# First batch's k and q loaded by groups of four heads, first attention block in two parts, attention times v in 64x64 tiles from block 8 and two blocks later, and new planner costs

## The chip, the cores and the metric

The kernel runs on one core of one Trainium2 chip. The metric is the device time in microseconds (us) of one execution, as the median of several runs. The engines are TensorE (PE, with its weight loads as PEld), VectorE (DVE), ScalarE (ACT), GpSimd (POOL) and SyncE (SP), which here issues nearly all DMAs.

## What is computed

Sliding-window attention, and then a two-layer feed-forward with a squared ReLU on its output:

```python
B, H, S, D = q.shape                                    # 8, 8, 576, 64
scores = np.matmul(q, k.transpose(0, 1, 3, 2)) / np.sqrt(D)
mask = np.abs(pos[:, None] - pos[None, :]) <= 32
scores = np.where(mask, scores, -1e9)
attn = np.exp(scores - scores.max(-1, keepdims=True))
attn = attn / (attn.sum(-1, keepdims=True) + 1e-9)
x = np.matmul(attn, v).transpose(0, 2, 1, 3).reshape(B * S, H * D)   # 4608 x 512
r = np.maximum(x @ w_in, 0.0)                           # 4608 x 2048
out = (s * (r * r) + b) @ w_out                         # 4608 x 512
```

All inputs and the output are float32 in DRAM. The kernel multiplies in bfloat16.

## The kernel before

The 4608 tokens are cut into 36 attention blocks of 128 tokens. A block's result is written, transposed, into a slot of the tile xt (512 features x 128 tokens). The feed-forward takes tokens in tiles of 128 (six tiles) and then 256 (fifteen). Its first product (line 1015) writes 512 columns of ht; ACT applies the ReLU (line 1024), DVE squares into gt (line 1043); the second product (line 1063) sums 16 matmuls per 128 tokens into one of the banks outp and ptp (in the last tiles also sc and av), DVE scales and adds the constant row cvec (line 1077), and SP stores. cvec is b times the column sums of w_out; the matmuls called quarters (line 940) need all of w_out. The feed-forward alone is 1344 + 592 matmuls. It fixes most of PE's work, and the rest of PE's time is attention, transposes and waiting.

Attention comes in three forms. (1) The first LIGHT = 3 blocks go through `attend_light`: scores and transposed scores are both computed, the row maxima are turned on PE and subtracted there, ACT takes the exponential of the transposed scores, and the normalised result is turned back (lines 691 to 782). (2) The other blocks go through `attend`: scores (line 820), a mask-and-maximum on DVE (line 832) and an exponential on ACT (line 840) for each of eight heads, a division by the row sums in two halves on POOL or DVE (line 854), and a transpose of the probabilities p into pts, on PE for the blocks below PDMA = 4 (line 877) and by a DMA after that (line 868). (3) The product with v is `av_one` for blocks below NOLD = 12: sixteen matmuls with 128 contracted rows, for which a copy vo of v shifted by 64 rows is made by `make_vo` (line 892). From block 12 on it is `av` in 64x64 tiles: 24 small matmuls into two banks (lines 909 and 915), one of which ACT copies to half (line 924) before DVE adds both into xt (line 926).

The first batch's k and q (blocks 0 to 3 use nothing else) come raw. Each is loaded in two halves, which split the 36 rows of a chunk: 16 chunks by 8 heads on the partitions (lines 571 and on). Each half is cast to bfloat16 (to parts of xt) and turned by matmuls with a permutation (line 593) into kwt and qwt, five banks for each. A block's scores need all five banks of both, and so all four loads. Later k and q are loaded in 128-token rows, cast (line 551, to kn and qn), and turned on PE up to block 11 (line 667, eight transposes each) and by a DMA after that.

The weights come in eight loads of 1 MB, i0 to i3 of w_in and o0 to o3 of w_out. Each is staged in a slot of gt (o2 in the output buffer) and cast in four pieces of 128x512. The order of the loads is the string FIRST: K and Q are the raw halves, `|` separates what is asked for before block 0, after block 0, after block 1 and so on. All loads are issued by SP in that order, each behind the one before it.

The order on every engine is worked out on the host, before launch, by a list scheduler (class `_Plan`). Every operation has a cost in ns for each engine that may run it, a latency, a key (its due position, mostly the token number minus a lead), and the resources that it reads and writes. On a free engine the ready operation of the smallest key goes next. An operation with several allowed engines is put where it would start and end first. The plan is then the fixed order of that engine: at run time each engine goes through its list and waits on semaphores, so an operation that comes late holds back everything behind it on its engine. A flag "small" on scores and tiled `av` makes the plan put them next to each other (HOLD, DEFER). Where the plan sees PE idle in the early stages it inserts dummy matmuls (`fill`, line 462).

Of the kernel before, what the change touches and what calls it, by code (L numbers as in the profile page):

```python
# [62 lines left out]
class _Plan:  # L63
# [39 lines left out]
    def order(self):  # L103
# [8 lines left out]
        def room(t, nd):  # L112

            while sum(q * min(1.0, (end - t) / dur) for end, dur, q in queue if end > t) + nd > RING:
                t += 50.0
            return t
# [15 lines left out]
        while len(out) < len(self.nodes):  # L132
# [13 lines left out]
            n = min(here, key=lambda m: (m.key, m.nid))  # L146
            if e == "pe":
# [123 lines left out]
def bass_sliding_window_symmetric__then__act_starrelu_kernel(  # L271
# [22 lines left out]
    CKEY, SKEY = 200, -9250  # L294
    SLOT = dict(i0=0, i1=1, i2=2, i3=3, o0=2, o1=3, o2=4, o3=2)
    RAWNS = 1450
    WHOLE, LIGHT, CH, NDIV = 4, 3, S // 16, 5
# [5 lines left out]
    AVK, NOLD, ONE, NVO = 384, 12, 11, 2  # L303

    def akey(j):
        return 128 * j - min(LEAD, L0 + LS * j)


    def CSET(j):
        return ("pool",)  # L310

    def VSET(j):
        return ("pool", "dve")

    def OSET(j):
        return ("act", "dve")

    with ExitStack() as es:
# [6 lines left out]
        def ps(shape, dt, nm):  # L325
# [16 lines left out]
        SS = [sb((128, 4, 128), F32, "ss") for _ in range(NS)]  # L342
        P = [sb((128, 8, 128), BF16, "p") for _ in range(NP)]
# [11 lines left out]
               for x, g in (("K", 0), ("Q", 8))}  # L355
        FLAT = {x: XT[:, :, :].rearrange("p a b -> p (a b)")[:, o:o + CH * D]
                for x, o in (("K", 0), ("Q", CH * D))}
# [3 lines left out]
        PICK = sb((128, 8, 128), BF16, "pick")  # L361
        EPS = sb((128, 128), BF16, "eps")
        M16 = [sb((128, 8, 2), BF16, "m16") for _ in range(2)]
        MT = [sb((16, 128), BF16, "mt") for _ in range(2)]
# [39 lines left out]
        def aff(dst, src, pat, base, cm, fill, rd, wr, key):  # L404
            add("pool", lambda e: e.affine_select(dst, src, pattern=pat, compare_op=ALU.is_ge,
                                                  fill=fill, base=base, channel_multiplier=cm),
                330, key, reads=rd, writes=wr)

        KC = K0 + 20
        for sg in (1, -1):  # L410
            src = ONES[:, 0:128] if sg == 1 else PERM[:, :]
            aff(PERM[:, :].rearrange("p (a g c) -> p a g c", a=2, g=NPAIR),
# [155 lines left out]
        def load_raw(x, half):  # L568
# [5 lines left out]
            if half:  # L574
                turn_raw(x)
# [568 lines left out]
```

## Time and profile before

| | |
|---|---|
| median of 3 runs | 319.31 us (319.23 to 321.96) |
| the profiled execution | 316.46 us |
| its span, first to last instruction | 314.7 us |
| granted clock of TensorE | 1.00 |
| PE busy | 300.8 us, 96% |
| DVE, ACT, POOL busy | 229.0, 230.0, 145.5 us |
| DMA | 61.82 MB, mean 196 GB/s |

The difference between the profiled execution and its span (1.8 us) lies before the first and after the last instruction. Times in the views count from the start of the span. In a row of the timeline stand the start, the length, the engine, the line, the operation, out<-in and the number of instructions merged, and in brackets the idle time before it with what ended it. Matmul rows overlap: the distance from one start to the next tells more than the length.

### The profile page before, as it was taken

Reading aid. Unit: us, or ns where it says so; the run is one execution under the profiler, and the core shown is the slowest. Engines: PE = TensorE matmul, PEld = TensorE weight load, DVE = VectorE, ACT = ScalarE, POOL = GpSimd, SP = SyncE. Lnnn points to the kernel's source line nnn. Section 1 sums busy time; section 2 is a strip of 40 time slices with the busy share of each in tenths; the row PEclk is TensorE's granted clock in tenths of the full one; section 3 lists DMA queues with packets and bytes.
Section 4 is the critical chain, followed back from the end, with each engine's and each line's share of the span. In section 5 each row is a group of like instructions: output and inputs, shape, how many; then the busy total and the mean of one; then the engine's idle time right before and its main releaser. Section 6 shows DMA issues by size and latency. Waiting matters only on the chain.

```text
span 314.7 us, 10141 instructions
## 1 busy us (share of the span) xinstructions
PE 300.8 (96%) x3936; PEld 207.4 (66%) x3981; DVE 229.0 (73%) x897; ACT 230.0 (73%) x747; POOL 145.5 (46%) x192
## 2 busy tenths in 40 slices
PE   7899899998999999999999999999999999999996
PEld 3468657586667665776666766666666666676674
DVE  5779499899998778677766787678858767653242
ACT  5577866899797868698787878798878778835230
POOL 7233476556575534445454654655654532220000
PEclk9999999999999999999999999999999999999999
DMA  7998999999999999999999999899999562220011
GB/s 273 359 351 228 361 268 214 240 229 179 210 213 210 232 187 197 223 227 176 191 218 226 210 205 233 217 192 226 225 247 204 123 149 70 70 67 35 33 69 68
DMA packets 157125, 61.82 MB, mean 196 GB/s; under 512 B 131220, under 2 KB 147988, under 8 KB 157076
## 3 DMA queue, kind: packets, MB, share of 16 engines
q1 hardware_dynamic: 157072, 61.16, 90.7%
q8 instruction: 31, 0.51, 0.7%
q14 instruction: 18, 0.15, 0.2%
q10 hardware_dynamic: 4, 0.00, 0.0%
HBM read 37.03 MB, written 9.44 MB: 148 GB/s over the span
## 4 chain that ended last, share of the span: by engine, by line
PE 77%; DMA 7%; DVE 7%; ACT 3%; POOL 2%; issue 2%; SPq 1%
PE ht L1015 35%; PE ptp L1063 15%; PE outp L1063 15%; DMA gt<-in_moe_w_out_dram 3%; PE sc L820 3%; DMA v<-in_v_dram 2%; ACT p L840 2%; PE sc L1063 2%; DMA r32k<-in_k_dram 2%; PE av L1063 2%; DVE ss L832 1%; PE tp L909 1%; PE av L915 1%; DVE mx L704 1%; DVE outs L1077 1%
## 5 line engine op out<-in xcount | busy, mean ns | idle before, releaser
L1015 PE MATMUL ht<-xt,win 128*128 128x256 bf16 (+1 forms) x1344 | 146.5, 257 | 0.0
L1015 PEld LDWEIGHTS ht<-xt,win 128*128 128x128 bf16 x1344 | 115.1, 98 | 32.7
L1024 ACT ACTIVATE r<-ht 128x512 bf16<-128x512 f32 x144 | 85.1, 592 | 47.3 <-PE ht L1015 45.8
L1043 DVE TENSOR_TENSOR gt<-r 128x512 bf16<-128x512 bf16 x144 | 83.6, 583 | 48.7 <-ACT r L1024 47.1
L840 ACT ACTIVATE p<-ss,mx 128x128 bf16<-128x128 f32 x264 | 110.0, 420 | 7.6 <-DVE mx L832 6.9
L854 POOL TENSOR_TENSOR p<-p,rc 128x512 bf16<-128x512 bf16 x64 | 70.0, 1114 | 77.5 <-DVE rc L849 77.5
L832 DVE CUSTOM_DVE_ANT_0 ss<-sc,mask 128x128 f32<-128x128 f32 x264 | 62.0, 280 | 8.8 <-PE sc L820 8.4
L1063 PE MATMUL outp<-wout,gt 128*128 128x512 bf16 (+1 forms) x246 | 63.0, 372 | 3.9 <-issue 1.7
L1063 PE MATMUL ptp<-wout,gt 128*128 128x512 bf16 x240 | 61.9, 379 | 1.7 <-issue 1.3
L840 ACT ACTIVATION_READ_ACCUMULATOR p<-ss,mx 128x1 f32 x264 | 50.2, 190 | 0.0
L1063 PEld LDWEIGHTS outp<-wout,gt 128*128 128x128 bf16 x272 | 24.9, 98 | 19.3 <-ACT wout L556 1.0
L1063 PEld LDWEIGHTS ptp<-wout,gt 128*128 128x128 bf16 x256 | 24.1, 98 | 19.3
L551 POOL CAST kn<-r32k 128x512 bf16<-128x512 f32 x34 | 21.1, 646 | 23.9 <-DMA r32k<-in_k_dram 23.9
L551 POOL CAST qn<-r32q 128x512 bf16<-128x512 f32 x32 | 21.3, 665 | 9.9 <-DMA r32q<-in_q_dram 9.5
L832 DVE DVE_READ_ACCUMULATOR2_ANT mx<- 128x1 f32 x264 | 20.8, 79 | 0.0
L924 ACT COPY half<-tp 128x512 f32<-128x512 f32 x24 | 14.0, 583 | 9.2 <-PE av L915 8.8
L551 POOL CAST ve<-v 128x512 bf16<-128x512 f32 x27 | 18.0, 667 | 3.3 <-PE av L915 2.5
L926 DVE TENSOR_TENSOR xt<-av,half 128x512 bf16<-128x512 f32 x24 | 16.3, 681 | 0.9 <-ACT half L924 0.8
L820 PEld LDWEIGHTS sc<-kt,qt 64*64 64x64 bf16 x768 | 10.8, 108 | 8.7 <-issue 7.8
L820 PE MATMUL sc<-kt,qt 64*64 64x64 bf16 (+1 forms) x768 | 14.2, 204 | 0.0
L846 DVE TENSOR_SCALAR sm<-sm 128x8 f32<-128x8 f32 x33 | 6.7, 202 | 8.9 <-ACT p L840 8.8
L1077 DVE SCALAR_TENSOR_TENSOR outs<-outp,scb,cvec 128x512 f32<-128x512 f32 (+1 forms) x17 | 12.4, 728 | 0.9 <-PE outp L1063 0.9
(142 smaller groups left out, 237.3 us busy)
## 6 DMA issues: line engine op xcount, KB each, us to landing
out_dram<-outs SPq DMA_DIRECT2D x35, 256.0 KB, 3.8
v<-in_v_dram SPq DMA_DIRECT2D x28, 256.0 KB, 5.5
r32q<-in_q_dram SPq DMA_DIRECT2D x28, 256.0 KB, 5.2
r32k<-in_k_dram SPq DMA_DIRECT2D x9, 512.0 KB, 4.7
gt<-in_moe_w_in_dram SPq DMA_DIRECT2D x4, 1024.0 KB, 10.6
gt<-in_moe_w_out_dram SPq DMA_DIRECT2D x3, 1024.0 KB, 9.7
v<-in_v_dram SPq DMA_DIRECT2D x8, 192.0 KB, 5.1
r32k<-in_k_dram SPq DMA_DIRECT2D x3, 448.0 KB, 4.8
```

The source lines that it names most:

```text
L551: return e.tensor_copy(dst, src)
L820: r = e.matmul(SC[hh][64 * u:64 * u + 64, pr, x0:x1], lhsT=qq, rhs=kk, start=True, stop=True)
L832: lambda e, ss=ss, x=x, y=y, pr=pr, hh=hh: e.tensor_tensor_reduce(out=SS[ss][:, x, :], in0=SC[hh][:, pr, :], in1=MASK[kind][:, :], scale=- ...
L840: lambda e, ss=ss, x=x, y=y: e.activation(P[pb][:, y, :].rearrange("q (a p t) -> q a p t", a=2, t=2), spread(SS[ss][:, x, :]), AF.Exp, bia ...
L854: return e.tensor_tensor(P[pb][:, y0:y0 + 4, :], P[pb][:, y0:y0 + 4, :], RC[mb][:, y0:y0 + 4].unsqueeze(2).broadcast_to([128, 4, 128]), AL ...
L924: add("act", lambda e: e.copy(HALF[hb][:, :], AV2[:, :]), 620, key + AVK, reads=[AV2N], writes=[("HALF", hb)])
L926: add("dve", lambda e: e.tensor_tensor(XT[:, :, 128 * (j % NX):128 * (j % NX) + 128], AV[:, :, :], HALF[hb][:, :].rearrange("p (a b) -> p ...
L1015: r = e.matmul(hbank[:, nt * f:nt * f + nt], lhsT=WIN[:, kc, 128 * ft:128 * ft + 128], rhs=XT[:, kc, x0:x0 + nt], start=(kc == 0), stop=(k ...
L1024: return e.activation(R1[rb][:, :], hbank[:, :], AF.Relu, bias=0.0, scale=1.0)
L1043: return e.tensor_tensor(d, r, r, ALU.mult)
L1063: r = e.matmul(op_[:, 0:cn], lhsT=GT[:, g_, fc, :], rhs=WOUT[:, fc, c0:c0 + cn], start=(fc == 0), stop=(fc == 15))
L1077: add("dve", lambda e, ob=ob, op_=op_, c0=c0, cn=cn: e.scalar_tensor_tensor(OUTS[ob][:, 0:cn], op_[:, 0:cn], SCB[:, 0:1], CVEC[:, c0:c0 + cn],
```

## The change

- **Raw k and q.** The first halves are now heads 0 to 3 and the second halves heads 4 to 7 (32 chunks by 4 heads on the partitions, 18 rows of each, the same bytes in each load). A half can be turned by itself: six groups of twelve matmuls for k and as many for q in place of five groups each. The order is Q0 K0 Q1 K1. The casts go to the buffers of ss and p rather than to xt.
- **Block 0** (`NSPLIT = 1`) is worked in two parts, heads 0 to 3 and heads 4 to 7, each with its own scores, maxima, exponential, product and normalisation. Block 1 is cut in the two sets of even and odd heads. The row sums now share a bank with the product. LIGHT falls from 3 to 2, so block 2 goes through `attend`.
- **Loads.** i0 goes ahead of v0 and v1; k2 and o0 go ahead of v3, q4 and v4; q5 ahead of o1. The slots of o0 and o1 are those that i0 and i1 leave.
- **AV.** `NOLD` falls from 12 to 8, so blocks 8 to 11 use 64x64 tiles and have no vo. `attend_av(j - 2)` is asked for after the scores of block j (DA = 2). PDMA rises from 4 to 5: block 4's probabilities are turned on PE.
- **Feed-forward.** Eight tiles of 128 and fourteen of 256; TAIL falls from 3 to 2.
- **Engines.** Weights may be cast on DVE too; v is cast on POOL alone (POOL or DVE before); k and q below block 8 on POOL or ACT (POOL before); vo also on POOL; the division on POOL alone from block 2 (NDIV 5 to 2); ReLU keys 400 ns earlier.
- **Costs.** Nearly all costs and latencies of the planner are new, mostly smaller costs and larger latencies, and the leads LEAD and LS, which makes a new order on every engine. The five dummy operations with the scalars s and b move from the head to after block 1.

In the order that the planner gives out, PE has 10 dummy matmuls (16 before), 144 matmuls of line 593 as before, 24 transposes of p (8 before), 96 matmuls of `av_one` (144 before), and 224 + 448 small ones of `av` (192 + 384 before).

```diff
-START, RING, ISSUE, LAND = 800.0, 2400.0, 700.0, 2000.0
+START, RING, ISSUE, LAND = 800.0, 2400.0, 700.0, 1200.0
-HOLD, DEFER, CHANGE = 800.0, 200.0, 97.0
+HOLD, DEFER, CHANGE = 200.0, 200.0, 97.0
-        n = _Node(len(self.nodes), eng, fn, cost, 300.0 if eng == "pe" else 130.0, key, dsem,
+        n = _Node(len(self.nodes), eng, fn, cost, {"pe": 300.0, "pool": 190.0}.get(eng, 230.0), key, dsem,
...
-    TILES = [128] * 6 + [256] * 15
+    TILES = [128] * 8 + [256] * 14
-    LEAD, L0, LS = 640, 600, 60
-    RELU, SQ = 500, 200
-    FIRST = "K0 K1 Q0 Q1 v0 v1 i0 i1 i2 v2 i3 v3 v4|q4 o0 k2 o1 o2 q5 o3|v5|||"
+    LEAD, L0, LS = 560, 600, 70
+    RELU, SQ = 900, 200
+    FIRST = "Q0 K0 Q1 K1 i0 v0 v1 i1 i2|v2 i3 k2 o0 v3 q4 q5 v4 o1 o2 o3||v5||"
-    WSET = {"i": ("pool", "act"), "o": ("act", "pool")}
-    NFLEX, TAIL = 8, 3
-    PDMA, KQDMA, AHEAD, GATE = 4, 11, 4, 5
-    SLOT = dict(i0=0, i1=1, i2=2, i3=3, o0=2, o1=3, o2=4, o3=2)
-    WHOLE, LIGHT, CH, NDIV = 4, 3, S // 16, 5
+    WSET = {"i": ("pool", "act", "dve"), "o": ("act", "pool", "dve")}
+    NFLEX, TAIL = 10, 2
+    PDMA, KQDMA, AHEAD, GATE = 5, 11, 4, 5
+    SLOT = dict(i0=0, i1=1, i2=2, i3=3, o0=0, o1=1, o2=4, o3=2)
+    RAWNS, NSPLIT = 1450, 1
+    WHOLE, LIGHT, CH, NDIV = 4, 2, S // 16, 2
-    AVK, NOLD, ONE, NVO = 384, 12, 11, 2
+    AVK, NOLD, ONE, NVO, DA = 384, 8, 11, 2, 2
     def CSET(j):
-        return ("pool",)
+        return ("pool",) if j >= 8 else ("pool", "act")
     def VSET(j):
-        return ("pool", "dve")
+        return ("pool",)
...
         def load_raw(x, half):
-            src = {"K": k, "Q": q}[x][0].rearrange("h (c r) d -> (h c) (r d)", r=CH)
+            src = {"K": k, "Q": q}[x][0].rearrange(
+                "h (c r) d -> (h c) (r d)", c=32)[128 * half:128 * half + 128, :]
...
-            if half:
-                turn_raw(x)
+            turn_raw(x, half)
...
-        def turn_raw(x):
+        def turn_raw(x, half):
+            step, n = CH * D // 8, CH // 6
+            ckey_, tkey = (-9500, -9400) if half == 0 else (HC, akey(0) - HT_)
+            banks = ([(TPF, "TP"), (HT[0], ("HT", 0)), (PTPF, "PTP")] if x == "K" else
+                     [(AVF, "AV"), (OUTP, ("OUTP", 0)), (HT[0], ("HT", 0))]) if half == 0 else [
+                         (HT[(i + (x == "Q")) % 2], ("HT", (i + (x == "Q")) % 2)) for i in range(3)]
...
+            split = j < NSPLIT
+            def sl(hh):
+                return slice(4 * hh, 4 * hh + 4) if split else slice(hh, 8, 2)
...
-                cost = {"dve": 620.0, "pool": 1000.0}
+                cost = {"dve": 610.0, "pool": 1050.0}
...
                 make_vo(j)
+                if DA and j - DA >= NOLD:
+                    attend_av(j - DA)
                 (attend_light if j < LIGHT else attend)(j)
...
+                if j == NT - 1:
+                    for x in range(max(NOLD, NT - DA), NT):
+                        attend_av(x)
```

More of the change, by code (lines that the diff above doesn't have):

```diff
@@ L112, in room @@
         def room(t, nd):
-            while sum(q * min(1.0, (end - t) / dur) for end, dur, q in queue if end > t) + nd > RING:
+            while sum(q for end, dur, q in queue if end > t) + nd > RING:
                 t += 50.0
@@ L574, in load_raw @@
[L574 to L586 removed]
+            lastload[0] = add("sp", lambda e: [e.dma_start(
+                RAW[x][:, lo:hi], src)], 500,
+                -LEAD - 2000, writes=[("RAW", x, half)] + stage(x, half),
+                dsem=f"dr{x}{half}", dtime=RAWNS + 500 * (x + str(half) == "K0"),
+                behind=lastload[0], ndesc=128)
```

376 lines of the change are left out of this document (216 added, 160 removed).

## The prediction

> **What bounds the kernel now.** I read the page's busy times first, then busy time by stage, then the PE timeline of the first 50 us with the casts that show when loads land, and last the waits of PE.
>
> ```profile
> span 314.7 us, 10141 instructions
> PE 300.8 (96%) x3936; PEld 207.4 (66%) x3981; DVE 229.0 (73%) x897; ACT 230.0 (73%) x747; POOL 145.5 (46%) x192
> ```
>
> ```profile
> 9.20:21.30 12.10, 10.31 (x230) 5.59 (x223) 8.18 (x21) 6.98 (x14) 4.40 (x8) 1.00 1.09 372
> 21.30:28.14 6.84, 6.84 (x160) 5.88 (x152) 6.72 (x17) 5.43 (x12) 2.65 (x5) 1.00 0.88 189
> 28.14:46.08 17.94, 16.00 (x252) 12.31 (x247) 13.36 (x45) 13.41 (x37) 9.80 (x15) 1.00 1.05 329
> 46.08:100.00 53.92, 51.72 (x736) 37.13 (x746) 49.79 (x197) 44.91 (x159) 32.62 (x41) 1.00 1.11 215
> 100.00:282.40 182.40, 179.66 (x2225) 123.20 (x2252) 133.76 (x577) 144.73 (x501) 89.47 (x109) 1.00 0.98 188
> ```
>
> In these rows the columns after the length are busy PE, PEld, DVE, ACT, POOL, then granted clock, DMA share and GB/s. From 100 us on PE is busy 179.66 of 182.40 us: only less work for PE can shorten that stage. Before 46 us matters are different. The first feed-forward matmul runs at 21.3 us, and the loads run at 372 and then 329 GB/s, except from 21.3 to 28.1 us, where 189 GB/s come in.
>
> ```profile
> 15.17 1.14 ACT L556 CAST win<-gt 128x512 bf16<-128x512 f32 x2 [3.08 <-DMA gt<-in_moe_w_in_dram]
> 24.27 1.14 ACT L556 CAST win<-gt 128x512 bf16<-128x512 f32 x2 [0.36 <-DMA gt<-in_moe_w_in_dram]
> 31.49 1.14 ACT L556 CAST wout<-gt 128x512 bf16<-128x512 f32 x2 [0.75 <-DMA gt<-in_moe_w_out_dram]
> 36.69 1.14 ACT L556 CAST wout<-gt 128x512 bf16<-128x512 f32 x2 [1.03 <-DMA gt<-in_moe_w_out_dram]
> 43.41 1.17 POOL L551 CAST wout<-gt 128x512 bf16<-128x512 f32 x2 [0.63 <-DMA gt<-in_moe_w_out_dram]
> 21.32 1.96 PE L1015 MATMUL ht<-xt,win 128*128 128x128 bf16 x32
> 26.22 1.07 PE L1015 MATMUL ht<-xt,win 128*128 128x128 bf16 x16
> 28.14 1.96 PE L1015 MATMUL ht<-xt,win 128*128 128x128 bf16 x32
> 29.94 0.17 PE L766 MATMUL tp<-ones,eps 128*128 128x8 bf16 x1
> 38.03 1.02 PE L1063 MATMUL outp<-wout,gt 128*128 128x512 bf16 x3 [0.88 <-POOL wout L551]
> 42.84 0.62 PE L667 MATMUL tp<-ident,qn 128*128 128x128 bf16 x8 [0.55 <-POOL qn L551]
> 46.08 1.05 PE L940 MATMUL tp<-wout,ones 128*32 128x512 bf16 x16
> ```
>
> A cast that waits for its DMA starts when the load lands: i0 at 15.2, i3 at 24.3, o0 at 31.5, o1 at 36.7, o3 at 43.4 us. PE's work follows them: the last quarter of the first tile at 26.2 after i3, a wait of 0.88 for o1's cast at 38.0, the sums over all of w_out at 46.1 after o3. That last row (line 940) is my mark. Ahead of it the loads set the pace, behind it PE does.
>
> **The change, part by part.** I take the distance to the mark, the work behind it, and the stalls behind it.
>
> *Head up to the first feed-forward matmul.* In the new order PE turns the first heads while the second half loads, and block 0's reduction, exponential and normalisation come in halves. Its four loads of raw k and q are as large as before, so the last lands when it did:
>
> ```profile
> 9.25 1.01 POOL L551 CAST xt<-gt 128x288 bf16<-128x288 f32 x2 [0.65 <-DMA gt<-in_q_dram]
> 11.64 0.11 PEld L691 LDWEIGHTS sc<-maskb,ident 128*128 128x128 bf16 x2 [0.73 <-DVE qwt L551]
> 12.67 1.29 DVE L704 TENSOR_REDUCE mx<-sc 128x4 f32<-128x512 f32 x2 [0.31 <-PE sc L696]
> 16.22 0.59 ACT L746 ACTIVATE pts<-ptp 128x512 bf16<-128x512 f32 x1
> 11.51 0.41 DVE L551 CAST ve<-v 128x512 bf16<-128x512 f32 x1
> 19.96 0.42 DVE L551 COPY xt<-tp 128x512 bf16<-128x512 bf16 x1 [0.37 <-PE tp L782]
> ```
>
> The last turns end by 11.6 as before. From there the second part saves one of two reductions (half of 1.29) and one exponential (0.59): 1.2 us off a path of 11.6 to 20.4. Against it, i0 now goes ahead of v0 and v1. The same bytes are then in by about 15.2, i0's old time, so v1 arrives there rather than before 11.5, and block 0's product cannot start before a cast of it, about 15.9. PE's in-order list has that product ahead of part two's subtraction of the maxima, so everything behind waits for v1. Bounds: 0 to 2.4 us earlier (the 1.2 twice over, if PE's shorter list doubles it); I take 1, so 20.3.
>
> It matters little, as the fourth quarter of w_in still lands at 24.3 (the same loads go ahead of i3). What counts is what PE has done when i3 is cast, about 25.4. The new list has 96 matmuls of line 1015 ahead of the next work on other tiles, from about 20.3. A group of 32 takes 1.80 us (28.14 to 29.94). The 32 that need i3 fit between 25.4 and 28.0 and the 64 others before it, so by 28.0 these 96 can be done, where before 64 were done at 28.14. Gain at this point: 1.8 us.
>
> *From there to the mark.* The old kernel still had to do 192 - 64 = 128 of these, the new one 208 - 96 = 112. Both have six groups of four matmuls of line 1063. The rest comes from the rows below, by distances between starts.
>
> ```profile
> 33.89 1.03 PE L1063 MATMUL ptp<-wout,gt 128*128 128x512 bf16 x4
> 34.75 0.61 PE L667 MATMUL tp<-ident,kn 128*128 128x128 bf16 x8
> 35.20 1.95 PE L1015 MATMUL ht<-xt,win 128*128 128x128 bf16 x32
> 86.49 0.32 PE L892 MATMUL av<-pts,ve 128*64 128x64 bf16 x8
> 86.86 0.45 PE L820 MATMUL sc<-kt,qt 64*64 64x128 bf16 x24
> 87.46 0.81 PE L1063 MATMUL outp<-wout,gt 128*128 128x512 bf16 x3 [0.16 <-issue]
> ```
>
> New: 112 x 1.80/32 = 6.3; six groups at 0.86, 5.2; two turns of k and q at 0.45, 0.9; two transposes of p at the same 0.45, 0.9; two products `av_one` at 0.37, 0.75; block 4's scores 0.6. That is 14.7 us of PE work, so PE alone would reach the mark at 42.7. The loads decide whether it may. At 350 GB/s, the middle of the stages beside it, the 189 GB/s stage is short of (350 - 189) x 6.84 = 1.10 MB, 3.1 us. In that stage the old list has v3, v4 and q4 in rows of one head each, with o0 asked for behind them; the new one asks for k2 and o0 there, with the small rows behind. I take half of the 3.1 as won: o3 at 41.8, cast by 43.0, the mark at 43.3. Bounds: 42.0 (all won, PE's list tightened by its missing dummies), and 45.2 if the load order wins nothing and only PE's lead is kept. Gain at the mark: **2.8 us, of 0.9 to 4.1**.
>
> Block 2's shorter way (`attend` in place of `attend_light`) is in that sum. It hides PE time only because ACT and DVE have room: 13.4 of 17.94 us each in this stage, and its eight exponentials add 8 x 0.42 = 3.4 us to ACT less two of 0.59. If that cover were gone, PE's transposes of p would wait up to 2.2 us.
>
> ```profile
> L840 ACT ACTIVATE p<-ss,mx 128x128 bf16<-128x128 f32 x264 | 110.0, 420 | 7.6 <-DVE mx L832 6.9
> L854 POOL TENSOR_TENSOR p<-p,rc 128x512 bf16<-128x512 bf16 x64 | 70.0, 1114 | 77.5 <-DVE rc L849 77.5
> L924 ACT COPY half<-tp 128x512 f32<-128x512 f32 x24 | 14.0, 583 | 9.2 <-PE av L915 8.8
> ```
>
> *Work behind the mark.* The new list has 16 fewer matmuls of line 1015 left: -0.9. Block 4's p is turned on PE: +0.45. Blocks 8 to 11 change `av_one` for the tiled product:
>
> ```profile
> 150.08 0.41 PE L820 MATMUL sc<-kt,qt 64*64 64x128 bf16 x22
> 150.71 1.05 PE L1015 MATMUL ht<-xt,win 128*128 128x256 bf16 x8
> ```
>
> Scores and tiled product together take 0.63 there, and one switch of 0.16, against 0.97 (86.49 to 87.46) with its switch: 0.18 for each of four blocks, -0.7, if they are put next to each other; apart a second switch takes it back. I take -0.5. One tile of 256 becomes two of 128, the same columns: nothing. Sum: **-0.9, of -1.2 to +0.3**. The two blocks of delay move no work.
>
> The Trainium skill ("TensorEngine Tiling (Array Packing)", PSUM Bottleneck) speaks against this part: tiling speeds up TensorE but not the reading of PSUM. The row of line 924 agrees: each such block adds an ACT copy of 0.58, four here, 2.3 us. They lie where ACT is busy 44.91 of 53.92 us, and eight copies to vo go away in turn, so I count nothing; by the rule alone it would be 2.3 us on a bound ACT.
>
> *Stalls behind the mark.* The longest is this:
>
> ```profile
> 77.58 0.62 PE L667 MATMUL tp<-ident,qn 128*128 128x128 bf16 x8 [1.04 <-POOL qn L551]
> ```
>
> k and q may now be cast on ACT too, and this place is left with shorter waits. I take -0.7; bounds -1.5 and +3, since POOL gets more to do (below). The end (last product, scaling, store) is the same work with four banks: nothing, +-0.3.
>
> **Sum:** -2.8 - 0.9 - 0.7 = -4.4 us. The profiled execution took 316.46, of which 1.8 lies outside the span, so 312.1. The median of the runs is 319.31, 2.85 above that execution; the same difference gives **314.9 us** for the median (-1.4%).
>
> **Rivals.**
>
> *No measurable change.* The same 13 MB of first loads pass through one queue, so o3 lands at 43.4 as before, and new waits on POOL eat the stall term. For it: 329 to 372 GB/s in most of the head. Against it: the 189 GB/s stage. It leaves 0.9 + 0.9 = 1.8 us: 317.5.
>
> *PE cools down.* With 10 dummies in place of 16, PE may be idle for long before the first feed-forward matmul.
>
> ```profile
> 1.33 3.17 PE L462 MATMUL ht<-ones 128*128 128x512 bf16 x7 [1.33 <-DVE nil L397]
> 6.35 0.39 PE L462 MATMUL ht<-ones 128*128 128x512 bf16 x1
> ```
>
> The first seven take 0.45 apiece, later ones of this width 0.215 (33.89 to 34.75 for four). If PE fell back once for as long as the first row, 3.17 us, it would lose 3.17 - 7 x 0.215 = 1.7 us, mostly ahead of i3's landing. Priced in full it gives 316.6. Against it: the granted clock is 1.00 throughout, and the list leaves work between the waits. The Trainium skill ("TensorE: Matmul & The Clock Gate", What's actually happening) has the clock fall to half after an idle window of about 3.4 us; by that rule the first row is the cold clock and the longest wait decides.
>
> *Slower: POOL holds PE.* All divisions from block 2 on, all casts of v and some of vo are now POOL's: four more at 1.11, nine more of v at 0.67, three of vo at about 0.6, less eight casts of weights at 0.61 to 0.80. That is some 6 us more, in a stage where its list alternates divisions with qn and kn, which PE's turns (line 667) wait for.
>
> ```profile
> L551 POOL CAST ve<-v 128x512 bf16<-128x512 f32 x27 | 18.0, 667 | 3.3 <-PE av L915 2.5
> ```
>
> Seven turns lie behind the mark. If each of them found one division (1.11) and one cast of v (0.67) ahead of its own cast, PE would lose 7 x 1.78 = 12.5 us less the 1.04 of before; with the gains at the mark and of the work kept (3.7) that is 319.3 - 3.7 + 11.5 = 327.1. It decides from about 0.7 us for each turn, where the gain is gone; from 1.1 it is slower by over 1%. Against it: POOL is busy 32.62 of 53.92 us there, and it can catch up.
>
> *More than forecast.* All of the 3.1 us of loads won, and the 2.2 us that PE is idle from 46 to 100 mostly gone: -4.1 - 1.2 - 1.5 = -6.8, 312.5.
>
> **How the numbers follow.** Forecast (312.6 to 316.1) 0.45; no measurable change 0.24 and the cool clock 0.05; more 0.13; POOL holds PE 0.13. A measurement of this kernel can tell about 1%, 3.2 us, from no change. Faster by over 1%: 0.45 + 0.13 = 0.58. Same: 0.24 + 0.05 = 0.29. Slower: 0.13. The range for 8 in 10 reaches from 311.0, the case "more" with the 1.5 us of its stall term once again, to 319.5, where only POOL holding PE is left out.
>
> **What would show it.** Right: line 986 (the new place of the sums over w_out) at 42 to 45 us; o0's casts by 29, not 31.5; fewer than 1.8 us waited by PE behind the mark; scores and tiled product adjacent for blocks 8 to 11; the same 179 us-like saturation from 100 us on. Wrong: a mark at 46 or later, a stage at 189 GB/s that has only moved, waits of PE on kn, qn or p from POOL, a granted clock below 1.

## The result, and the profile after

The changed kernel takes 317.41 us (median of 20 runs, 316.58 to 318.34) against 318.80 of the kernel before beside it (20 runs, 316.49 to 321.96): a ratio of 0.9957, 95% interval 0.9939 to 0.9975. That is 1.4 us less, clear of no change among these runs, but within 1%. The profiled execution took 317.1 us. Ratios leave out executions more than 1.5% above the fastest of their kernel, medians do not: the ratio of v ahead of i0 below rests on four of twelve executions, that of the dummies with the old loads on two of six, and from the three profiles among those left out (these two kernels and the first with the AV part alone) only the last one's times up to its mark are used. The page of the changed kernel, its head and the clock row of its 40 slices:

```profile
span 315.4 us, 10283 instructions
PE 302.6 (96%) x3992; PEld 212.0 (67%) x4041; DVE 227.7 (72%) x917; ACT 228.7 (73%) x762; POOL 150.2 (48%) x194
...
PEclk9957999999999999999999999999999999999999
```

Busy time by stage of the changed kernel (after the length: busy PE, PEld, DVE, ACT, POOL, then granted clock, DMA share, GB/s); 48.96 is the mark, the sums over all of w_out, now line 986:

```profile
9.20:16.90 7.70, 6.58 (x148) 4.24 (x142) 6.27 (x16) 3.67 (x8) 3.33 (x5) 0.99 1.10 354
16.90:27.00 10.10, 9.86 (x157) 7.25 (x158) 7.28 (x36) 6.75 (x18) 3.56 (x6) 0.50 1.12 305
27.00:48.96 21.96, 19.78 (x313) 16.09 (x312) 21.26 (x76) 17.05 (x57) 13.26 (x14) 1.00 0.98 267
48.96:100.00 51.04, 49.61 (x772) 36.42 (x784) 42.00 (x171) 40.87 (x142) 30.70 (x39) 1.00 1.13 210
100.00:282.40 182.40, 179.92 (x2270) 124.14 (x2298) 134.75 (x579) 145.11 (x510) 93.77 (x115) 1.00 0.99 190
```

Two things stand out. For ten microseconds TensorE ran at half clock, although it was busy 9.86 of 10.10 us; the mean clock was 0.978 to 0.989 in all 20 runs. And from 27 us to the mark DVE was busy 21.26 of 21.96 us, where the stage before the old mark had 13.36 of 17.94. PE's rows in that part:

```profile
23.49 1.89 PE L1091 MATMUL ht<-xt,win 128*128 128x128 bf16 x16
26.94 1.96 PE L1091 MATMUL ht<-xt,win 128*128 128x128 bf16 x32
28.96 3.00 PE L1091 MATMUL ht<-xt,win 128*128 128x128 bf16 x48
32.84 0.22 PE L1017 MATMUL tp<-sc,ones 1*128 1x2 bf16 x3 [0.88 <-DVE sc L1008]
43.37 0.81 PE L1141 MATMUL outp<-wout,gt 128*128 128x512 bf16 x3 [1.25 <-DVE mx L871]
48.96 1.05 PE L986 MATMUL tp<-wout,ones 128*32 128x512 bf16 x16
```

The first feed-forward matmul starts at 23.49 (21.32 before), and the mark is at 48.96 (46.08 before): 2.9 us later, not 2.8 earlier. What lies behind the mark fell from 314.7 - 46.08 = 268.6 to 315.4 - 48.96 = 266.4 us. Between the first feed-forward matmul and the mark PE waits twice for DVE, and never for a load: 0.88 for the scalars that moved here from the head, and 1.25 where the row names a maximum of the attention (line 871) and the waiting matmuls also read o1, whose last two pieces DVE cast from 41.47 to 43.05. Waits of PE behind the mark:

```profile
PE ptp L1141 <- issue: 1.6, 10, 0.2
PE outp L1141 <- issue: 1.1, 7, 0.2
```

Only switches between large and small matmuls are left, 17 of them; the 1.04 us for qn are gone.

**The kernel before varies more than its first profile told.** It was profiled once more, unchanged: 319.3 us, span 317.6.

> The kernel before unchanged, profiled once more. If its first profile (316.46 us, mark at 46.08) was one of its faster executions, an execution near its median of 318.8 has its mark at 47 to 48.5 us and the same 268 to 269 us behind it: then the mark moved by less than the 2.9 us that the two profiles show. If the difference lies behind the mark, the mark is again at 46.

Its stage 9.20 to 14.00, its first feed-forward matmul and its mark, then its waits of PE from 160 to 180 us:

```profile
9.20:14.00 4.80, 3.97 (x84) 2.12 (x84) 3.04 (x8) 2.89 (x5) 1.01 (x2) 0.71 1.13 348
```

```profile
22.51 1.96 PE L1015 MATMUL ht<-xt,win 128*128 128x128 bf16 x32
...
47.02 1.05 PE L940 MATMUL tp<-wout,ones 128*32 128x512 bf16 x16
```

```profile
PE tp L909 <- DMA pts<-p: 2.2, 2, 1.2
```

Both theories hold in part: the mark is 0.9 us later, after a short dip of the clock, and 2.2 us are waited for two DMA transposes of p. So the 46.08 of the prediction came from one of its shorter executions (316.46 against a median near 319). The medians of the kernel before were 317.4 to 319.3 over the groups of runs below; ratios from different groups that differ by half a per cent aren't told apart.

### The profile page after: what moved, and what is told of

The parts are those of the page before. It is cut to its first block, busy times and chain, and to the rows that moved or that the text cites. A ratio compares the mean times of both kernels' runs of the same rounds, so it can differ in the third digit from the quotient of the medians.

```text
span 315.4 us, 10283 instructions
## 1 busy us (share of the span) xinstructions
PE 302.6 (96%) x3992; PEld 212.0 (67%) x4041; DVE 227.7 (72%) x917; ACT 228.7 (73%) x762; POOL 150.2 (48%) x194
## 4 chain that ended last, share of the span: by engine, by line
PE 89%; DVE 5%; issue 2%; DMA 2%; ACT 1%; SPq 0%; POOL 0%; DVEq 0%
PE ht L1091 39%; PE outp L1141 19%; PE ptp L1141 18%; PE sc L859 4%; DMA gt<-in_q_dram 2%; PE tp L955 1%; DVE gt L1119 1%; PE av L961 1%; PE sc L1141 1%; PE tp L677 1%; DVE wout L554 1%; PE sc L719 1%; PE av L938 1%; PE av L1141 1%; PE sc L709 0%
## 5 line engine op out<-in xcount | busy, mean ns | idle before, releaser
L1091 PEld LDWEIGHTS ht<-xt,win 128*128 128x128 bf16 x1408 | 117.0, 98 | 31.0 <-DVE xt L972 0.4
L879 ACT ACTIVATE p<-ss,mx 128x128 bf16<-128x128 f32 x272 | 113.3, 420 | 8.4 <-DVE mx L871 8.1
L893 POOL TENSOR_TENSOR p<-p,rc 128x512 bf16<-128x512 bf16 x68 | 75.5, 1130 | 75.5 <-DVE rc L888 74.0
L1141 PE MATMUL outp<-wout,gt 128*128 128x512 bf16 (+1 forms) x262 | 67.7, 373 | 3.3 <-DVE mx L871 1.3
L871 DVE CUSTOM_DVE_ANT_0 ss<-sc,mask 128x128 f32<-128x128 f32 x272 | 64.7, 281 | 7.5 <-PE sc L859 7.5
L1141 PE MATMUL ptp<-wout,gt 128*128 128x512 bf16 x251 | 65.0, 379 | 2.2 <-issue 1.6
L1141 PEld LDWEIGHTS outp<-wout,gt 128*128 128x128 bf16 x288 | 27.0, 98 | 19.9 <-ACT r L1100 1.2
L1141 PEld LDWEIGHTS ptp<-wout,gt 128*128 128x128 bf16 x272 | 25.4, 98 | 21.3
L554 POOL CAST ve<-v 128x512 bf16<-128x512 f32 x37 | 25.3, 686 | 20.8 <-PE av L961 17.9
L970 ACT COPY half<-tp 128x512 f32<-128x512 f32 x28 | 16.4, 585 | 14.2 <-PE av L961 13.9
L972 DVE TENSOR_TENSOR xt<-av,half 128x512 bf16<-128x512 f32 x28 | 19.1, 682 | 4.4 <-ACT half L970 4.4
```

The lines of the kernel that those rows point to most:

```text
L554: return e.tensor_copy(dst, src)
L871: lambda e, ss=ss, x=x, y=y, pr=pr, hh=hh: e.tensor_tensor_reduce(out=SS[ss][:, x, :], in0=SC[hh][:, pr, :], in1=MASK[kind][:, :], scale=- ...
L879: lambda e, ss=ss, x=x, y=y: e.activation(P[pb][:, y, :].rearrange("q (a p t) -> q a p t", a=2, t=2), spread(SS[ss][:, x, :]), AF.Exp, bia ...
L893: return e.tensor_tensor(P[pb][:, y0:y0 + 4, :], P[pb][:, y0:y0 + 4, :], RC[mb][:, y0:y0 + 4].unsqueeze(2).broadcast_to([128, 4, 128]), AL ...
L970: add("act", lambda e: e.copy(HALF[hb][:, :], AV2[:, :]), 482, key + AVK, reads=[AV2N], writes=[("HALF", hb)])
L972: add("dve", lambda e: e.tensor_tensor(XT[:, :, 128 * (j % NX):128 * (j % NX) + 128], AV[:, :, :], HALF[hb][:, :].rearrange("p (a b) -> p ...
```

## The experiments

Each ratio is to the kernel before beside it, with its 95% interval. "Behind" is the span less the mark.

### The AV part

Undone in the changed kernel:

```diff
-    AVK, NOLD, ONE, NVO, DA = 384, 8, 11, 2, 2
+    AVK, NOLD, ONE, NVO, DA = 384, 12, 11, 2, 0
```

> The changed kernel with the AV part undone: NOLD = 12 and DA = 0, so blocks 8 to 11 use sixteen matmuls and a copy of v again and nothing is asked for two blocks late. If the time behind the mark that the change won (268.6 to 266.4 us) comes from the AV part: behind the mark 0.5 to 1.5 us longer, time 318 to 319. If it comes from the 16 matmuls of the feed-forward that are already done and from fewer waits: unchanged within 0.4 us.

319.76 us, 1.0020 (0.9995 to 1.0045). The mark stays (49.00), behind it 268.2 instead of 266.4. Its waits of PE behind the mark:

```profile
PE ptp L1141 <- issue: 1.9, 12, 0.2
PE outp L1141 <- issue: 1.7, 11, 0.2
PE outp L1141 <- DVE mx L871: 0.2, 1, 0.2
```

So this part is worth about 1.8 us in the trace. Half of it is seen here: 23 switches for 3.6 us instead of 17 for 2.7. The kernel before had 18; the five more come with the rest of the change, and this part takes them away again. Without this part nothing is left of the gain.

The part alone on the kernel before (with `attend_av` split off and called as in the change), and once more:

```diff
-    AVK, NOLD, ONE, NVO = 384, 12, 11, 2
+    AVK, NOLD, ONE, NVO, DA = 384, 8, 11, 2, 2
```

> The kernel before with the AV part alone: 64x64 tiles from block 8, two blocks late; head, loads and divisions as before. Theory A (the AV part is the whole gain, the head and its loads give nothing): about 2 us below before, 316.8, with the mark (sums over w_out) where before has it, 46 to 48 us, and 266 to 267 us behind it. Theory B (the head's change and the AV part gain together, for example through the divisions on POOL): at most 0.5 us below before.

> The kernel before with the AV part alone once more, for a profile of an ordinary execution and a second ratio: 0.989 to 0.995, mark 46 to 47, 267 to 269 us behind it. If the ratio is above 0.996, the first one was luck.

317.26 us, 0.992 (0.989 to 0.995); again 317.09 us, 0.9983 (0.9952 to 1.0014). The second is the bad case named in advance: the two disagree because the kernel before took 319.29 and 317.44 beside them. The time itself is that of the changed kernel. Behind the mark the second profile has 268.3 us, against 268.6 and 270.6 in the two profiles of the kernel before, so on the old head the traces leave open whether the part is worth 0.3 or 2.2 us there. The second execution that was profiled shows something else, which is taken up under the clock.

### The clock

19 dummy matmuls in the changed kernel, behind the scores, transposed scores and subtractions of blocks 0 and 1:

```diff
+                if (j, hh, part) in ((0, 1, 1), (1, 0, 0), (1, 1, 0)):
+                    warm(e, r, 2)
...
+            def warm(e, r, n):
+                fill(e, "attn", n)
+                return r
```

> The changed kernel with 19 more dummy matmuls (128x512 into the free bank ht) put behind matmuls that are in the list anyway, between block 0's second part and the first feed-forward matmul; order and loads are as in the changed kernel. Clock theory (the half clock from 16.9 to 27.0 us is what makes the mark, the sums over all of w_out, late): granted clock 1.00, first feed-forward matmul at 21 to 22 instead of 23.5 us, mark at 46 to 47 instead of 49.0, and 2 to 3 us off the time (314.5 to 315.5). Load theory (o1 landing at 38.9 and o3 at 45.7 make it late): clock 1.00 too, but o3 still at 45.7, the mark still at 48 to 49, and the time within 1 us of the changed kernel's 317.4.

318.13 us, 0.9983 (0.9961 to 1.0006). The clock is full, and yet the first feed-forward matmul is at 24.68 and the mark at 49.92:

```profile
18.00:24.68 6.68, 6.39 (x103) 3.48 (x100) 4.59 (x13) 3.09 (x7) 1.93 (x4) 1.00 1.15 296
...
30.00:49.92 19.92, 17.65 (x268) 13.54 (x264) 19.35 (x66) 15.30 (x50) 11.81 (x12) 1.00 0.95 270
```

The dummies cost 19 x 0.215 = 4.1 us of PE at full clock, in a list that is nearly full, so this run cannot show what the full clock alone is worth. With four of them, 0.9 us:

```diff
+                if (j, hh, part) in {(0, 1, 1): 1, (1, 0, 0): 1}:
+                    warm(e, {(0, 1, 1): 1, (1, 0, 0): 1}[(j, hh, part)])
...
+                if (j, hh, part) in {(0, 1, 1): 2}:
+                    warm(e, {(0, 1, 1): 2}[(j, hh, part)])
```

> The changed kernel with four dummy matmuls of 512 columns between the scores of blocks 0 and 1 (19 before: these held the clock at 1.00 and gained nothing). Theory A (the half clock costs time, the 19 took it back): clock 1.00, mark 1 to 2 us earlier than 48.96, about 316. Theory B (other engines set the pace ahead of the mark): mark within 0.5 us of 48.96 whatever the clock, 317 to 318.

316.79 us, 0.9946 (0.9909 to 0.9984). The half clock comes three microseconds later but comes (1.00 from 18 to 20 us, 0.52 from 20 to 22, 0.50 to 26), first feed-forward matmul 22.52, mark 48.41. Half a microsecond: neither theory is told apart by that.

The other way round, the kernel before without its nine dummies behind the first seven:

```diff
-FILL, FILL_MIN, FILL_SHARE, FILL_NS = ("attn", "sums"), 400.0, 0.5, 220.0
+FILL, FILL_MIN, FILL_SHARE, FILL_NS = ("sums",), 400.0, 0.5, 220.0
```

> The kernel before with the dummy matmuls of the attention stage left out but for the first seven. Clock theory: the granted clock falls to half somewhere between 8 and 25 us and the time rises by 1 to 3 us, with the mark at 47 to 49 instead of 46.1. If the dummies were not what holds the clock: clock 1.00 and the time within 0.5 us of the kernel before.

318.95 us, 1.0002 (0.9969 to 1.0034), clock 0.984, first feed-forward matmul 23.31, mark 47.92. The head cools; it is 2.0 us longer than in the first profile of the kernel before and 0.8 longer than in the second, and the median does not move. Nine dummies are 1.9 us less for PE, which may pay for it. The cleanest case came unasked. The kernel with the AV part alone has the head of the kernel before, with its dummies, and most of its runs had a clock of 1.00; the profiled one of its second measurement had 0.984. A stage of it, then its first feed-forward matmul and its mark:

```profile
18.00:26.00 8.00, 8.00 (x109) 5.60 (x106) 4.79 (x13) 3.42 (x7) 3.80 (x7) 0.50 0.99 270
```

```profile
23.64 3.60 PE L1029 MATMUL ht<-xt,win 128*128 128x128 bf16 x32
...
48.55 1.05 PE L947 MATMUL tp<-wout,ones 128*32 128x512 bf16 x16
```

In its first profile the same program ran its head at full clock:

```profile
18.00:26.00 8.00, 7.71 (x176) 5.70 (x171) 7.07 (x18) 5.66 (x11) 3.78 (x7) 1.00 0.98 264
```

```profile
21.41 2.12 PE L1029 MATMUL ht<-xt,win 128*128 128x128 bf16 x32
...
46.90 1.05 PE L947 MATMUL tp<-wout,ones 128*32 128x512 bf16 x16
```

The stretch at half clock goes with 2.2 us more up to the first feed-forward matmul and 1.7 at the mark. Of the 2.2, 0.4 were there when the clock fell at 18.0 us (the sums of line 766 start at 17.74 against 17.37).

The 20 executions of the changed kernel say the same. Eight had a mean clock of 0.978 and took 317.95 us in the mean, eleven had 0.983 or 0.984 and took 317.2, one had 0.989 and took 316.6. Over 315 us these clocks mean about 14, 10 and 7 us at half clock, so some 3.5 us more of it go with about 0.7 us. Carried on in proportion, the 10 us of an ordinary execution would be worth about 2 us. That is an estimate; no execution of this kernel kept the full clock.

### The loads

The old order and slots in the changed kernel:

```diff
-    FIRST = "Q0 K0 Q1 K1 i0 v0 v1 i1 i2|v2 i3 k2 o0 v3 q4 q5 v4 o1 o2 o3||v5||"
+    FIRST = "Q0 K0 Q1 K1 v0 v1 i0 i1 i2 v2 i3 v3 v4|q4 o0 k2 o1 o2 q5 o3|v5|||"
-    SLOT = dict(i0=0, i1=1, i2=2, i3=3, o0=0, o1=1, o2=4, o3=2)
+    SLOT = dict(i0=0, i1=1, i2=2, i3=3, o0=2, o1=3, o2=4, o3=2)
```

> The changed kernel with the loads asked for in the old order (v0 and v1 ahead of i0; v3, v4 and q4 ahead of o0 and k2; o1, o2, q5, o3) and the old staging slots. The planner makes its order anew. Load theory: o1 lands near 36.7 and o3 near 43.4 as before, the mark is at 46 to 47 us, the time 2 to 3 us below the changed kernel (314.5 to 315.5), whatever the clock does. Clock theory: the clock still falls to half after about 17 us, the mark stays at 48 or later, the time within 1 us of 317.4.

321.81 us, 1.0106 (1.0067 to 1.0146); first feed-forward matmul 25.41, o1 at 36.8, o3 at 45.0, mark 52.12. With both edits, this and the 19 dummies:

> Both edits together: the 19 dummies and the old load order. If the two causes add up: clock 1.00, o3 near 43.4, mark at 45 to 46, time 313.5 to 315. If one cause alone counts, the time is that of the better of the two single edits.

325.69 us, 1.0117 (1.0046 to 1.0189): no better. Here the dummies did not hold the clock: five executions had 0.974 to 0.984 and took 324.80 to 327.76 us, one had 1.00 and took 320.58. The new order and slots alone in the kernel before:

```diff
-    FIRST = "K0 K1 Q0 Q1 v0 v1 i0 i1 i2 v2 i3 v3 v4|q4 o0 k2 o1 o2 q5 o3|v5|||"
+    FIRST = "K0 K1 Q0 Q1 i0 v0 v1 i1 i2|v2 i3 k2 o0 v3 q4 q5 v4 o1 o2 o3||v5||"
-    SLOT = dict(i0=0, i1=1, i2=2, i3=3, o0=2, o1=3, o2=4, o3=2)
+    SLOT = dict(i0=0, i1=1, i2=2, i3=3, o0=0, o1=1, o2=4, o3=2)
```

> The kernel before with the new order of first loads and the new staging slots of w_out alone. By the prediction's step: o3 lands at about 41.8 instead of 43.4 to 44.2, the mark comes 1 to 2 us earlier, time 1 to 2 us below before. Theory B (the small rows of q4, q5, v4 now stand ahead of o1 to o3 and hold the queue): o1 and o3 land 1 to 2 us later than before, the mark at 47 to 49, time at or up to 2 us above before.

322.80 us, 1.0103 (1.0053 to 1.0152). i0 ahead of v0 and v1 shows at once, in the first product of block 0 and the first feed-forward matmul (17.66 and 21.32 before):

```profile
19.52 0.34 PE L757 MATMUL av<-ve,pts 128*64 128x64 bf16 x5
...
23.14 1.07 PE L1015 MATMUL ht<-xt,win 128*128 128x128 bf16 x16
```

The mark is at 46.52, but only 160 instead of 192 matmuls of line 1015 are done there, and o3 lands at 44.7 instead of 43.4. Each order of loads goes with its own kernel: exchanged, both cost 1%. Why is not shown. The load step of the prediction is wrong on the old head, where o3 came later, not earlier. In the changed kernel o1 ahead of v4, o2 ahead of q5:

```diff
-    FIRST = "Q0 K0 Q1 K1 i0 v0 v1 i1 i2|v2 i3 k2 o0 v3 q4 q5 v4 o1 o2 o3||v5||"
+    FIRST = "Q0 K0 Q1 K1 i0 v0 v1 i1 i2|v2 i3 k2 o0 v3 q4 o1 v4 o2 q5 o3||v5||"
```

> The changed kernel with the big loads of w_out set between the loads of small rows (o0, v3, q4, o1, v4, o2, q5, o3 in place of o0, v3, q4, q5, v4, o1, o2, o3). Load theory: o1 lands near 35 to 36 us, o3 near 44, the mark at 46.5 to 47.5, the time 1.5 to 2.5 us below 317.4. Vector-queue theory: o1 lands earlier but its casts on DVE still start behind other work, the mark stays at 48 to 49.5, the time within 0.7 us of 317.4.

317.39 us, 0.9962 (0.9927 to 0.9996). o1 lands 4.0 us earlier (34.9 instead of 38.9), o3 2.7 earlier (43.0 instead of 45.7), and the mark is at 50.15, in an execution that was the longest of its twelve (320.06 us, 13.7 us at half clock). The median is that of the changed kernel: these loads do not set its time. And v0, v1 ahead of i0, with the four dummies:

```diff
-    FIRST = "Q0 K0 Q1 K1 i0 v0 v1 i1 i2|v2 i3 k2 o0 v3 q4 q5 v4 o1 o2 o3||v5||"
+    FIRST = "Q0 K0 Q1 K1 v0 v1 i0 i1 i2|v2 i3 k2 o0 v3 q4 q5 v4 o1 o2 o3||v5||"
```

> The changed kernel with the four dummies and with v0 and v1 asked for ahead of i0 again. Beside it stands the run with the four dummies alone (0.9946 of before, first feed-forward matmul 22.5 us, mark 48.41). Theory A (the first product waits for v1, which lands at 14.2 us instead of 10.2): first feed-forward matmul 1 to 2 us earlier, mark 47 or earlier, 0.989 to 0.992. Theory B (what paces the stage lies behind that product): mark within 0.5 us of 48.4, 0.993 to 0.997.

324.04 us, 1.0060 (1.0007 to 1.0113), with runs from 318.45 to 324.78. The gain expected by theory A is not there. The three executions with a mean clock of 0.995 took 318.45 to 319.40 us, the nine at 0.968 to 0.979 took 322.65 to 324.78. The edit also changed the order on PE (a part of block 1's scores now stands ahead of block 0's second subtraction), so what is slower in it is not told apart.

### The elementwise engines

w_out cast on ACT and POOL alone in the changed kernel:

```diff
-    WSET = {"i": ("pool", "act", "dve"), "o": ("act", "pool", "dve")}
+    WSET = {"i": ("pool", "act", "dve"), "o": ("act", "pool")}
```

> The changed kernel with the casts of w_out on ACT and POOL alone, as before the change; the planner makes its order anew. Vector-queue theory (o1 lands at 38.9 us but DVE casts its two pieces only from 41.5 to 43.1, so PE waits 1.25 us and the mark comes 3.3 us after o3's landing): DVE busy ahead of the mark falls from 97% to under 90%, casts of o1 end within 2 us of its landing, the mark comes at 46 to 47.5 instead of 49.0, the time 1.5 to 2.5 us below the changed kernel's 317.4. Load theory (the landings of o1 and o3, 2.2 us later than before, are what counts): o3 still near 45.7, the mark at 48 or later, the time within 0.7 us of 317.4.

318.17 us, 0.9963 (0.9937 to 0.9989), mark 49.05. DVE is relieved, and PE waits for it all the same, once at another place:

```profile
27.00:49.05 22.05, 19.81 (x307) 16.16 (x307) 18.89 (x64) 17.89 (x57) 15.32 (x20) 0.99 0.98 266
```

```profile
32.92 0.22 PE L1017 MATMUL tp<-sc,ones 1*128 1x2 bf16 x3 [0.88 <-DVE sc L1008]
36.96 0.32 PE L938 MATMUL av<-pts,ve 128*64 128x64 bf16 x8 [1.04 <-DVE pts L554]
```

This edit, the order of loads with o1 ahead of v4, and the four dummies, all as shown above, together:

> The changed kernel with three single edits together: the four dummies, w_out cast on ACT and POOL alone, and o1 asked for ahead of v4, o2 ahead of q5. Each alone left the mark at 48.4 to 50.2. Theory A (several limits lie close behind one another, so that each alone hides behind the others): mark at 45 to 47, 314 to 315.5. Theory B (none of the three sets the pace): mark at 48 or later, 317.

317.15 us, 0.9937 (0.9909 to 0.9965), mark 49.38, clock 0.984. DVE is down to 17.15 of 22.38 us and PE still busy 20.26 of them. The clock still fell, so of theory A only casts and loads are refuted: neither sets the pace, alone or together, while PE's list itself nearly fills the stage. The profiled execution was the longest of the twelve; the two with a clock of 0.994 and 1.00 took 316.33 and 315.85 us.

### The forms of the first blocks

Block 0 in one part of eight heads in the changed kernel (`NSPLIT = 0`), block 2 through `attend_light` in the changed kernel (`LIGHT = 3`), and block 2 through `attend` in the kernel before (`LIGHT = 2`):

```diff
-    RAWNS, NSPLIT = 1450, 1
+    RAWNS, NSPLIT = 1450, 0
```

```diff
-    WHOLE, LIGHT, CH, NDIV = 4, 2, S // 16, 2
+    WHOLE, LIGHT, CH, NDIV = 4, 3, S // 16, 2
```

```diff
-    WHOLE, LIGHT, CH, NDIV = 4, 3, S // 16, 5
+    WHOLE, LIGHT, CH, NDIV = 4, 2, S // 16, 5
```

> The changed kernel with block 0 in one part of eight heads again (NSPLIT = 0); loads, order and AV as changed. Theory A (the split's chain of small steps through VectorE delays the first feed-forward matmul): first feed-forward matmul before 22.5 us, mark at 47 to 48, 316 us. Theory B (the split is worth what it was forecast to give, one reduction and one exponential): 0.5 to 1.2 us later, 318.

> The changed kernel with block 2 back in the form attend_light (LIGHT = 3): eight mask-and-maximum operations (0.28 us each) and two divisions less for DVE and POOL ahead of the mark, 2.3 us more for PE. Vector-queue theory: DVE has room again, the mark comes no later than 49.0 although PE has more to do, time within 1 us of 317.4 or below it. If PE's work is what counts ahead of the mark: mark near 51, time 319 to 320.

> The kernel before with block 2 alone in the way of the later blocks (LIGHT = 2). By the prediction's step (ACT and DVE have room, TensorE saves its way through scores_t, flip and less): mark 0.5 to 2 us earlier, time 0.5 to 2 us below before. Theory B (VectorE and ScalarE have no such room in that stage): DVE busy over 90% from 25 us to the mark, mark 0 to 2 us later, time at or above before.

The first gives 321.33 us, 1.0071 (1.0039 to 1.0102), first feed-forward matmul 26.60; the second 324.90 us, 1.0166 (1.0118 to 1.0214), mark 53.49; the third 317.63 us, 0.9965 (0.9935 to 0.9994), mark 46.31 with 160 of the matmuls of line 1015 done. In the changed kernel the two parts are worth 3.9 us of the medians and block 2's shorter way 7.5; in the second run the half clock also lasted 20.5 us instead of 10.2, so not all of the 7.5 is block 2's own. Block 2 (the last of these edits) and the AV part, both on the kernel before, should then add up:

> The kernel before with the AV part and block 2 in the later way, head and loads as before. The AV part alone gave 0.992 of before. If block 2 in this way gains on the old head, 0.986 to 0.990 of before (about 315); if it costs there, 0.994 or more.

320.65 us, 1.0057 (1.0035 to 1.0080): each alone was at or below the kernel before, and both together are slower, with the mark at 46.37 as for block 2 alone and all of the loss behind it (272.2 against 269.2). Of the kernels run, those with 316.8 to 317.4 (the changed one, with four dummies, with o1 ahead of v4, with all three edits, the AV part alone) can't be ranked.

## Why the prediction was wrong

The changed kernel was forecast at 314.9 us, -4.4; it takes 317.41, -1.4 against the median beside it. The step that failed is the first one, the head up to the first feed-forward matmul, and with it the gain of 2.8 us at the mark. Execution against execution the miss is larger: 317.1 against 316.46 is 0.6 us slower. The forecast added 2.85 us from the profiled execution to the median; beside the changed kernel that difference is 2.3 for the kernel before and 0.3 for the changed one, and 0.6 - 2.3 + 0.3 gives the -1.4. So the gain of the medians does not mean that part of the forecast for the head came true.

**Head: first feed-forward matmul at 20.3, measured 23.49.** The shorter work of block 0 was counted rightly in kind: unsplit, the same kernel gets there at 26.60. What was missing is the half clock from 16.9 to 27.0 us. The prediction had it as a rival of 0.05, "PE cools down", priced at 1.7 us, and argued from a granted clock of 1.00 before and a list with work between the waits. The work is there, PE is busy 6.58 of 7.70 us ahead of the dip, but most of it is small matmuls of 64 columns or in 64x64 tiles, a few with 8 rows, beside six of 512 columns, with no dummy among them. In one and the same program the dip went with 2.2 us at this place, and the executions of the changed kernel give about 2 for the whole time. That leaves about 1 of the 3.2 us, for which the runs name no single cause; the clock itself can have cost at most 3.4 here, half of the 6.8 us from its fall at 16.7 to 23.49. No run here held the clock in the changed head without adding work to PE, so the 2.2 is shown on the old head alone. The Trainium skill ("TensorE: Matmul & The Clock Gate", What's actually happening) has the clock fall after an idle window of about 3.4 us; the prediction took the longest wait as what decides by it. The traces do not agree: from 9.2 us to the dip the changed kernel's PE is never idle for over 0.54 us at a time, and in the kernel with the AV part alone the clock fell with no wait ahead of it longer than 0.85 us since the first dummies. How much of the array is in use may count; no run here settles that.

**96 matmuls done by 28.0, measured 31.96.** The 3.2 us of the head, and 0.8 more because the first 16 ran at half clock: the next work (line 754) starts at 25.17, so they took 1.68 us, against 0.9. An earlier head alone would not have mended all of it: i3 landed at 25.3, not 24.3, and DVE cast two of its pieces only from 27.24 to 27.99. The last 48 of the 96, which begin with the quarter that needs i3, take 2.7 us, so with these casts where they are the 96 end at 30.7 at best, 1.3 us earlier. Whether the casts would move with the head no run shows.

**From there to the mark: 15.3 forecast, 17.0 measured.** PE's own work was counted well, 14.7 us forecast; 17.0 less 0.88 and 1.25 of waits is 14.9. The waits are the other miss: "ACT and DVE have room" was read from a stage of 13.4 of 17.94, and the change put casts of w_in and w_out (5.0 us) and the scalars (2.4 us) there, until DVE was busy 21.26 of 21.96 us. The maxima are 16 against 13; block 2's eight ran ahead of this stage, at 23.6 to 25.4 us. Some of these rows:

```profile
L871 DVE CUSTOM_DVE_ANT_0 ss<-sc,mask 128x128 f32<-128x128 f32 x16 | 3.8, 280 | 0.0
L554 DVE CAST wout<-gt 128x512 bf16<-128x512 f32 x7 | 3.4, 532 | 0.0
...
L1008 DVE CAST sc<-sc 1x2 bf16<-1x2 f32 x3 | 1.3, 419 | 0.0
L1011 DVE TENSOR_TENSOR sc<-sc,sc 1x2 f32<-1x2 f32 x2 | 1.1, 563 | 0.0
```

Part of this is stretched rather than more. Two operations on two numbers each took 0.98 and 0.99 us beside two divisions of p on POOL. They end at 31.52 and 32.78, the divisions at 31.52 and 32.77, and PE's wait of 0.88 is for the second:

```profile
30.54 0.98 DVE L1011 TENSOR_TENSOR sc<-sc,sc 1x2 f32<-1x2 f32 x1
31.79 0.99 DVE L1008 CAST sc<-sc 1x2 bf16<-1x2 f32 x1
30.48 2.29 POOL L893 TENSOR_TENSOR p<-p,rc 128x512 bf16<-128x512 bf16 x2 [1.45 <-DVE sc L1008]
```

With `LIGHT = 3`, where no division ran beside them, the five such operations took 0.14 to 0.16 us each, and PE did not wait for them. In the runs with w_out cast on ACT and POOL and with all three edits the divisions stand beside them again, and a wait of 0.9 is there again. That points at the divisions, which the change put on POOL alone from block 2 on; no run took them off POOL or moved the scalars back, so their price is not shown.

Together 3.2 + 0.8 + 1.7 = 5.7 us: the distance from 43.3 to 48.96.

**Loads: o3 at 41.8, measured 45.7.** Wrong by 3.9 us, and without effect on this kernel: PE waits for no load between its first feed-forward matmul and the mark, and o3 at 43.0 did not bring the mark forward. The stage of low load rate that the prediction wanted to see go has moved, to 30 to 34 us; it was named there as a sign against the forecast. Another sign failed too: o0 landed at 30.4 and its first cast ran at 32.04, not by 29.

```profile
30.00:34.00 4.00, 3.12 (x54) 2.77 (x52) 4.00 (x15) 3.27 (x11) 3.52 (x3) 1.00 0.92 151
```

**Work behind the mark: -0.9 forecast for all of it, stalls -0.7; measured -2.2 together.** The direction is right. The AV term was mis-sized: -0.5 forecast, 1.8 us measured. The 0.18 us for each of four blocks makes 0.7 by the forecast's own rows, and the forecast let second switches take part of it back; in fact, against the same plan without this part, six switches of 0.16 us go away as well, 0.9. Against the kernel before it is one switch, and the rest of the change is worth only -0.4 behind the mark (268.6 to 268.2), where the forecast had -0.9 for 16 matmuls, -0.7 for the stalls and +0.45 for block 4. Of the four new tiled products the first three stand next to scores, as the forecast hoped, and the fourth, at 110.79 us, apart. The Trainium skill's rule against tiling ("TensorEngine Tiling (Array Packing)", PSUM Bottleneck), weighed there at 2.3 us, did not decide: the copies to half rose to 28, and this part is still the gain.

```profile
L970 ACT COPY half<-tp 128x512 f32<-128x512 f32 x28 | 16.4, 585 | 14.2 <-PE av L961 13.9
```

**The rivals.** "No measurable change" (317.5) is what came, but not by its mechanism: the loads are not what held the mark. "POOL holds PE" did not happen in its form; no wait of PE for kn, qn or p is left behind the mark, and what the divisions may hold, by way of DVE, lies ahead of it. "PE cools down" happened in every run of the changed kernel, its price close to what was written. "More" lacked both of its halves.

**The base.** The sum was made against a profiled execution with its mark at 46.08; another had 47.02 and 2.2 us of waits for transposes. Against that one the new mark is 1.9 us later and the part behind it 4.1 us shorter. It is not known how often those waits come.

What stays open: why the first feed-forward matmul is late by a further microsecond, what makes the clock fall, and why parts that gain alone lose together. Every edit makes the planner write a new order for all engines, so no run changed one thing only.

## What to carry to other kernels

Before a head gets shorter, count which matmuls keep the array busy in it: a row of busy PE that consists of small tiles is no evidence that the clock stays up, and where dummies go the clock has to be read again. "That engine has room" must be summed again with everything that the change puts into the stage, also the small operations that only move, and with what they take beside the work of the other engines. Where a scheduler writes the order, the parts of a change cannot be priced one by one; measure each of them undone and alone, profile the base twice, and compare executions with executions and medians with medians.

## What the hardware showed

- The granted clock fell to 0.50 for 10 us after a stage in which PE was busy 6.58 of 7.70 us, and one program fell so in one profiled execution and not in another. Every fall ahead of the mark that was profiled lasted 3.4, 6.8, 10.2, 13.7 or 20.5 us by the clock record of its trace, multiples of one step of 3.41.
- DVE's cast of 128x512 from f32 took 0.41 us in the head of the kernel before, and in the changed one two took 1.58 us at 41.47, while POOL cast too, in 0.80 instead of about 0.6. One POOL cast took 2.55:

```profile
32.72 2.55 POOL L554 CAST ve<-v 128x512 bf16<-128x512 f32 x1
41.21 0.80 POOL L554 CAST wout<-gt 128x512 bf16<-128x512 f32 x1
45.70 0.62 POOL L554 CAST wout<-gt 128x512 bf16<-128x512 f32 x1 [2.93 <-DMA gt<-in_moe_w_out_dram]
```

- A DMA transpose of p, usually hidden, came late by 0.95 and 1.20 us in one execution of the kernel before.
- Behind the mark of the changed kernel the 58 squares of 128x512 on DVE (line 1119) with POOL idle took at most 0.43 us each, those beside a division on POOL up to 1.32.
